# Batch 0's softmax ahead of the first weight conversions, and exponentials by head on ScalarE, in a fused attention and two-FFN kernel

## The chip, the cores and the metric

The program runs on one core of a Trainium2 chip. A core has TensorE (PE in the profile; its weight loads are PEld), VectorE (DVE), ScalarE (ACT), GpSimd (POOL) and SyncE (SP), which here issues the DMAs. Each engine works through its own instructions in a fixed order. The metric is the device time of one execution in microseconds (us), the median of several runs.

## The reference

Three stages, one behind the other, in float32. An attention over 8 batches, 8 heads, 576 positions and 64 values per head, in which the keys and values are first averaged over groups of eight positions; then a feed-forward layer with a leaky ReLU; then a gated feed-forward layer behind an RMS norm.

```python
k_p = k.reshape(B, H, Sp, pool, D).mean(axis=3)          # Sp = 72
v_p = v.reshape(B, H, Sp, pool, D).mean(axis=3)
scores = scale * np.matmul(q, k_p.transpose(0, 1, 3, 2))
scores = scores - np.max(scores, axis=-1, keepdims=True)
attn = np.exp(scores)
attn = attn / (np.sum(attn, axis=-1, keepdims=True) + 1e-09)
return np.matmul(attn, v_p)
...
h = x @ w_in                      # 4608 tokens, 512 -> 2048
g = np.maximum(0.01 * h, h)
return g @ w_out                  # 2048 -> 512
...
xn = x / np.sqrt(np.mean(x * x, axis=-1, keepdims=True) + 1e-06) * rms_g
g = xn @ w_gate                   # 512 -> 1536
return (g / (1 + np.exp(-g)) * (xn @ w_val)) @ w_out2
```

The weights arrive as float64.

## The kernel before

**Products.** Every large product is made of three TensorE products: each operand is split into a high part, rounded to a shorter float format, and a low part, the rest. `split` (L89 to L95) makes the two: a copy on ScalarE (L92) and a subtraction on VectorE or GpSimd (L95).

**Attention.** A batch has five tiles of queries (`t` = 0 to 4). Of each tile, step `t` transposes the queries (`qt`, `qT`), step `s` makes the scores and the softmax, step `x` transposes the softmax to `at` and `atr`, and the steps `av0` and `av1` multiply by the pooled values and write the tokens `xhl`. The steps `kp` and `vp` pool keys and values (`vs`, masked to `vm`, split to `vb`).

In `step_s` (L313) the scores of four heads stand in one PSUM bank (`sc`, two buffers under the tag `att`), 288 columns. For each half VectorE takes the maximum of each head (L331) and subtracts it (L332). Then one ScalarE instruction makes the exponentials of all eight heads, 576 columns (L336), VectorE sums them (L337), adds the small constant (L338), takes the reciprocal (L339) and multiplies (L340).

**Weights of the first layer.** `Weights` loads each 512 KB piece as pairs of 32-bit words (`raw_i` of w_in, `raw_o` of w_out) and makes a float of them. `begin` does one pass on ScalarE (L139, by the helper at L98) and one on VectorE (L141); `end`, one step later, combines the two on VectorE (L149) and splits the result (L92, L95; the subtraction on GpSimd for one piece, on VectorE for the next). A call of `W1.step` ends one piece and begins the next. Pieces are loaded into slots that earlier data leave. The last eight pieces, half as large, go through three buffers (tag `raw`) that batch 1's keys and values pass through too.

**First layer.** The 4,608 tokens are 9 tiles of 512, of which tile `j` = 0 holds batch 0. For each of 16 blocks `f` of w_in, `h_unit` (L597) makes `h` with 12 matmuls per 512 columns, then ScalarE makes `ghl` and `g` and VectorE their difference (L605); `y_unit` (L611) multiplies by w_out. Tile 0 runs its first 256 columns for `f` = 0 to 7, then all 512 columns for `f` = 8 to 15, then the other 256 columns for `f` = 0 to 7. Attention of the next batches and conversions run beside it.

**What sets the order.** In the first layer a scheduler that goes by its own timeline orders each engine's queue; the order written in the source is only one of its inputs. `keep_in_program_order` ties an instruction behind the one that was written just before it on its engine. In the second layer the written order is kept.

Of the kernel before, what the change touches and what calls it, by code (L numbers as in the profile page):

```python
# [8 lines left out]
F32 = mybir.dt.float32  # L9
# [3 lines left out]
AF = mybir.ActivationFunctionType  # L13
ALU = mybir.AluOpType
AX = mybir.AxisListType
# [7 lines left out]
def pooled_attention_then_two_ffns(  # L23
# [13 lines left out]
    nc = tc.nc  # L37
    B, H, S, D = q.shape
    NT, DM = out.shape
    P = 128  # L40
# [22 lines left out]
    ESCALE = 1.0 / (POOL * float(D) ** 0.5)  # L63
# [33 lines left out]
    def prelu(out, in_, alpha, scale=1.0):  # L97
        return nc.scalar.activation(out=out, in_=in_, func=AF.Prelu, scale=scale, alpha=alpha)  # L98
# [8 lines left out]
    class Weights:  # L107
# [25 lines left out]
        def begin(self):  # L133
            x = self.loaded.pop(0)
            t = x[2]
            top, low = t[:, :, 1], t[:, :, 0]


            prelu(top.bitcast(F32), top.bitcast(F32), 2.0 ** 32, scale=2.0 ** -112)  # L139

            nc.vector.tensor_scalar(  # L141
                out=low, in0=low.bitcast(U32), scalar1=0.9374 * 2.0 ** -29, scalar2=None, op0=ALU.mult
            )
            self.begun.append(x)

        def end(self):
# [22 lines left out]
    ap = att.__enter__()  # L169
# [5 lines left out]
    for h, sign in ((0, -1), (1, 1)):  # L175
        nc.gpsimd.affine_select(
            out=mask_main[:, h:h + 1], in_=mask_main[:, h:h + 1], compare_op=ALU.is_ge, fill=0.0,
# [4 lines left out]
    for sign, base in ((1, 0), (-1, REST - 1)):  # L182
        nc.gpsimd.affine_select(
            out=group, in_=group, compare_op=ALU.is_ge, fill=0.0, base=base, channel_multiplier=sign,
# [4 lines left out]
        out=mask_rest[:, :, 1], in_=group.rearrange("p d q -> p q d"), axis=AX.X, op=ALU.add  # L189
# [58 lines left out]
    def v_prep(b, r):  # L248
        rest = r >= NP
        n = R3 if rest else P  # L250
        x = vraw.pop((b, r))[0:n]
        vs = ap.tile([P, D], F32, tag="vs", bufs=2, name=f"vs{b}_{r}")[0:n]
        if b == 0:
            nc.vector.tensor_reduce(
                out=vs, in_=x.rearrange("p (r d) -> p d r", r=POOL), axis=AX.X, op=ALU.add
            )
        else:
            pool_sum(x)
            nc.gpsimd.tensor_tensor(out=vs, in0=x[:, 0:D], in1=x[:, D:2 * D], op=ALU.add)
        m = mask_rest.rearrange("p q h -> p (q h)") if rest else mask_main  # L260
        c = m.shape[1]
        vm = ap.tile([P, 4, D], F32, tag="vm", bufs=1, name=f"vm{b}_{r}")[0:n, 0:c]
        nc.gpsimd.tensor_tensor(
            out=vm, in0=vs.unsqueeze(1).to_broadcast([n, c, D]),
            in1=m.unsqueeze(2).to_broadcast([n, c, D]), op=ALU.mult,
        )
        if rest:

            t = ap.tile([R3, 4, D], F32R, tag="vbr", bufs=2, name=f"vb{b}_{r}")
            nc.scalar.activation(out=t, in_=vm, func=AF.Copy)  # L270
            z = slice(2 * R1, 3 * R1)
            nc.vector.tensor_tensor(out=t[z], in0=vm[z], in1=t[z].bitcast(F32), op=ALU.subtract)
        else:
            t = ap.tile([P, 2, 2, D], F32R, tag="vb", bufs=4, name=f"vb{b}_{r}")
            split(nc.scalar, t[:, HI], nc.vector, t[:, LO], vm)
        vb[b, r] = t
# [36 lines left out]
    def step_s(b, t):  # L313
        y = qT.pop((b, t))
        if b == 0:
            e = per.tile([P, H, SP], F32, tag=f"w{20 + t % 4}", bufs=1, name=f"ex{b}_{t}")
        else:
            e = ap.tile([P, H, SP], F32, tag="ex", bufs=1, name=f"ex{b}_{t}")
        st = ap.tile([P, 3, H], F32, tag="st", bufs=2, name=f"st{b}_{t}")
        n = 2 * SP  # L320
        for half in range(2):
            pt = bank("att", 2, f"sc{b}_{t}_{half}")
            for i in range(2):
                p = 2 * half + i
                nc.tensor.matmul(  # L325
                    pt[:, i * n:(i + 1) * n], y[:, p, :], kblk[b % 2][:, p * n:(p + 1) * n],
                    start=True, stop=True,
                )
            s = pt[:, 0:2 * n].rearrange("p (h c) -> p h c", h=4)
            hs = slice(4 * half, 4 * half + 4)  # L330
            nc.vector.tensor_reduce(out=st[:, 0, hs], in_=s, axis=AX.X, op=ALU.max)  # L331
            nc.vector.tensor_tensor(  # L332
                out=e[:, hs, :], in0=s, in1=st[:, 0, hs].unsqueeze(2).to_broadcast([P, 4, SP]),
                op=ALU.subtract,
            )
        nc.scalar.activation(out=e, in_=e, func=AF.Exp, scale=ESCALE)  # L336
        nc.vector.tensor_reduce(out=st[:, 1, :], in_=e, axis=AX.X, op=ALU.add)  # L337
        nc.vector.tensor_scalar(out=st[:, 1, :], in0=st[:, 1, :], scalar1=1e-9, scalar2=None, op0=ALU.add)  # L338
        nc.vector.reciprocal(out=st[:, 2, :], in_=st[:, 1, :])  # L339
        nc.vector.tensor_tensor(  # L340
            out=e, in0=e, in1=st[:, 2, :].unsqueeze(2).to_broadcast([P, H, SP]), op=ALU.mult
        )
        ex[b, t] = e
# [236 lines left out]
        W1.load()  # L580
    for x in before:
        run_step(x)
        if x[0] in "sx" and x[2] > 0:
            W1.step()

    gp = {}
# [675 lines left out]
```

## Time and profile before

| | |
|---|---|
| median of 3 runs | 1808.96 us (1805.79 to 1812.09) |
| the profiled execution | 1812.26 us, of which the span from first to last instruction is 1810.5 us |
| PE busy | 1758.0 us, 97% of the span |
| DVE, ACT, POOL busy | 891.1, 670.4, 551.2 us |

The page divides the span into 40 slices of 45 us. PE is busy for three tenths of the first and eight tenths of the second, and nine or more in all others, while DVE is at seven and nine tenths in these two and near five later. What is not TensorE's work therefore lies mostly in the first 90 us, and that stretch has to be read for itself.

### The profile page before, as it was taken

The page shows a single profiled execution, that of the slowest core. Times are in us where ns is not written, and L with a number is a line of the kernel's source. Part 1 is how long each engine was busy: PE and PEld are TensorE (multiplying, and loading weights), DVE is VectorE, ACT ScalarE, POOL GpSimd, SP SyncE. Part 2 cuts the span into 40 slices and gives each one's busy share as a digit, 9 for nine tenths or more (in the row PEclk, how much of TensorE's full clock was granted, in tenths as well). Part 3 has the DMA queues.
Part 4 walks back from the last instruction along what each step waited for, and adds up shares of the span by engine and source line. Part 5 has one row for each costly group of instructions (what it writes and reads, how often), then busy time and mean ns, then how long its engine had stood idle before and what let it go on. Part 6 is the DMA issues. An engine that isn't in the chain of part 4 may idle for free.

```text
span 1810.5 us, 23634 instructions
## 1 busy us (share of the span) xinstructions
PE 1758.0 (97%) x8596; PEld 1498.0 (83%) x8596; DVE 891.1 (49%) x1603; ACT 670.4 (37%) x1424; POOL 551.2 (30%) x681
## 2 busy tenths in 40 slices
PE   3899999999999999999999999999999999999999
PEld 2889887878888888888888888899788889978887
DVE  7974435454356555455344345345534444553331
ACT  5754333443344444344343332243232323322220
POOL 2653303334125142211110442154144204413320
PEclk6999999999999999999999999999999999999999
DMA  8833204447365555435451766687775668776562
GB/s 253 307 109 89 55 21 143 157 140 230 101 189 157 163 157 162 145 125 180 157 172 45 234 195 211 228 300 245 255 245 196 193 226 314 245 250 224 186 209 93
DMA packets 175555, 330.81 MB, mean 183 GB/s; under 512 B 54352, under 2 KB 90192, under 8 KB 174928
## 3 DMA queue, kind: packets, MB, share of 16 engines
q1 hardware_dynamic: 175440, 329.31, 56.1%
q8 instruction: 68, 1.11, 0.3%
q14 instruction: 47, 0.39, 0.1%
HBM read 277.87 MB, written 51.38 MB: 182 GB/s over the span
## 4 chain that ended last, share of the span: by engine, by line
PE 89%; DVE 5%; DMA 3%; issue 1%; ACT 1%; SPq 1%; POOL 1%; ACTq 0%; DVEq 0%; POOLq 0%
PE y L628 20%; PE h L592 20%; PE o L1089 16%; PE yg L1014 6%; PE yv L1014 6%; PE xv L1014 4%; PE xg L1014 4%; PE wg L1014 4%; PE wv L1014 4%; PE sc L325 2%; PE av L395 1%; PE xt L369 1%; DMA wo<-wo 1%; PE qt L303 1%; DMA y<-ye 1%
## 5 line engine op out<-in xcount | busy, mean ns | idle before, releaser
L592 PE MATMUL h<-xhl,w_i 128*128 128x512 f32 (+1 forms) x1824 | 438.2, 385 | 3.1 <-ACT xhl L92 1.3
L592 PEld LDWEIGHTS h<-xhl,w_i 128*128 128x128 f32 x1824 | 329.5, 191 | 68.3 <-DVE xhl L95 4.1
L1089 PE MATMUL o<-wo,u 128*128 128x512 f32 x1296 | 315.1, 390 | 3.5 <-DMA wo<-wo 3.4
L628 PE MATMUL y<-ghl,w_o 128*128 128x512 f32 (+1 forms) x1296 | 285.1, 365 | 1.4 <-DVE ghl L605 1.4
L1089 PEld LDWEIGHTS o<-wo,u 128*128 128x128 f32 x1296 | 242.0, 188 | 53.0 <-DMA wo<-wo 4.9
L628 PEld LDWEIGHTS y<-ghl,w_o 128*128 128x128 f32 x1296 | 218.9, 191 | 35.1 <-DVE ghl L605 1.8
L605 DVE TENSOR_TENSOR ghl<-g,ghl 128x512 fp32r<-128x512 f32 (+1 forms) x152 | 114.6, 754 | 241.5 <-ACT g L98 238.3
L98 ACT ACTIVATE ghl<-h 128x512 fp32r<-128x512 f32 (+1 forms) x152 | 87.0, 572 | 233.4 <-PE h L592 232.9
L628 PE MATMUL y<-ghl,wr 128*128 128x512 f32 x624 | 158.9, 395 | 0.0
L628 PEld LDWEIGHTS y<-ghl,wr 128*128 128x128 f32 x624 | 115.1, 188 | 22.4
L95 POOL TENSOR_TENSOR u<-e2g,u 128x512 fp32r<-128x512 f32 (+1 forms) x25 | 29.7, 1190 | 308.3 <-ACT u L92 308.3
L229 POOL TENSOR_TENSOR v<-v 128x256 f32<-128x256 f32 (+2 forms) x84 | 59.7, 713 | 107.6 <-DMA v<-in_v_dram 105.0
L98 ACT ACTIVATE g<-h 128x512 f32<-128x512 f32 (+1 forms) x152 | 86.8, 571 | 1.0 <-DVE ghl L605 1.0
L1014 PE MATMUL yg<-T,ag 128*128 128x512 f32 (+1 forms) x360 | 84.0, 368 | 0.0
L1014 PE MATMUL yv<-T,av 128*128 128x512 f32 (+1 forms) x360 | 83.8, 368 | 0.0
L1014 PE MATMUL xg<-xa,ag 128*128 128x512 f32 (+1 forms) x360 | 83.8, 367 | 0.0
L1014 PE MATMUL xv<-xa,av 128*128 128x512 f32 (+1 forms) x360 | 83.7, 367 | 0.0
L1014 PEld LDWEIGHTS yg<-T,ag 128*128 128x128 f32 x360 | 66.0, 188 | 10.0 <-DVE e1v L991 0.6
L1014 PEld LDWEIGHTS yv<-T,av 128*128 128x128 f32 x360 | 66.2, 188 | 9.5
L1014 PEld LDWEIGHTS xv<-xa,av 128*128 128x128 f32 x360 | 66.0, 188 | 9.6
L1014 PEld LDWEIGHTS xg<-xa,ag 128*128 128x128 f32 x360 | 66.1, 188 | 9.4
L735 POOL TENSOR_TENSOR parts_g<-raw_g,parts_g 128x256 fp32r<-128x256 f32 (+1 forms) x48 | 33.7, 727 | 102.7 <-ACT parts_g L731 102.7
(166 smaller groups left out, 2596.2 us busy)
## 6 DMA issues: line engine op xcount, KB each, us to landing
wo<-wo SPq DMA_DIRECT2D x120, 512.0 KB
av<-op_v SPq DMA_DIRECT2D x90, 512.0 KB
ag<-op_g SPq DMA_DIRECT2D x90, 512.0 KB
wr<-wo SPq DMA_DIRECT2D x52, 512.0 KB
y<-ye SPq DMA_DIRECT2D x36, 256.0 KB
op_g<-parts_g SPq DMA_DIRECT2D x36, 256.0 KB
op_v<-parts_v SPq DMA_DIRECT2D x36, 256.0 KB
out_dram<-oe SPq DMA_DIRECT2D x36, 256.0 KB
```

What stands on the lines that cost most here:

```text
L95: lo_eng.tensor_tensor(out=lo, in0=src, in1=hi.bitcast(F32), op=ALU.subtract)
L98: return nc.scalar.activation(out=out, in_=in_, func=AF.Prelu, scale=scale, alpha=alpha)
L229: nc.gpsimd.tensor_tensor(out=x[:, :n], in0=x[:, :n], in1=x[:, n:2 * n], op=ALU.add)
L303: nc.tensor.transpose(pt[:, c * P:(c + 1) * P], x[:, c * P:(c + 1) * P], ident)
L325: nc.tensor.matmul(pt[:, i * n:(i + 1) * n], y[:, p, :], kblk[b % 2][:, p * n:(p + 1) * n], start=True, stop=True,)
L369: nc.tensor.transpose(pt[:, c * P:(c + 1) * P], e[:, c, 0:P], ident)
L592: nc.tensor.matmul(pt, w[:, sp, c * P:(c + 1) * P], x[:, mp, c, :], start=c == 0 and i == 0, stop=c == n_k - 1 and i == 2,)
L605: nc.vector.tensor_tensor(out=t[:, LO, :], in0=g, in1=t[:, HI, :].bitcast(F32), op=ALU.subtract)
L628: nc.tensor.matmul(pt, w[:, sp, m * P:(m + 1) * P], g[:, mp, a - c0:a - c0 + n], start=ydone[j, a] == 1 and i == 0 and m % per_bank == 0, ...
L735: own(nc.gpsimd.tensor_tensor(out=d[:, :, LO, :], in0=x, in1=d[:, :, HI, :].bitcast(F32), op=ALU.subtract))
L1014: nc.tensor.matmul(pt, wt[:, a, c, sp, :], xt[:, mp, :], start=start and c == 0 and i == 0, stop=c == 1 and i == 2, skip_group_check=not s ...
L1089: nc.tensor.matmul(pt, u[:, sp, m * P:(m + 1) * P], w[:, mp, :], start=f == 0 and i == 0, stop=f == F2 - 1 and i == 2,)
```

## The change

There are three edits.

1. The two instructions of `begin` are tied behind what is written just before them on ScalarE and on VectorE. And `W1.step` is called behind other steps of batch 0: before, behind `s` of tile 1 and `x` of tile 1; now, behind `s` of tile 1, `x` of tiles 0 and 1 and each of the four `av0`, seven calls in all where there were two.
2. For batches 0 and 1 the subtraction, the single exponential and the sum are replaced. The maximum is scaled by -ESCALE (in two small VectorE instructions per tile), and ScalarE makes one exponential per head, 72 columns, straight from the scores, with that number as bias, and gives the head's sum as well.
3. `vs` has four buffers instead of two, `vm` two instead of one.

```diff
-            prelu(top.bitcast(F32), top.bitcast(F32), 2.0 ** 32, scale=2.0 ** -112)
+            x1 = prelu(top.bitcast(F32), top.bitcast(F32), 2.0 ** 32, scale=2.0 ** -112)
-            nc.vector.tensor_scalar(
+            x2 = nc.vector.tensor_scalar(
                 out=low, in0=low.bitcast(U32), scalar1=0.9374 * 2.0 ** -29, scalar2=None, op0=ALU.mult
             )
+            tc.keep_in_program_order(x1)
+            tc.keep_in_program_order(x2)
...
-        vs = ap.tile([P, D], F32, tag="vs", bufs=2, name=f"vs{b}_{r}")[0:n]
+        vs = ap.tile([P, D], F32, tag="vs", bufs=4, name=f"vs{b}_{r}")[0:n]
...
-        vm = ap.tile([P, 4, D], F32, tag="vm", bufs=1, name=f"vm{b}_{r}")[0:n, 0:c]
+        vm = ap.tile([P, 4, D], F32, tag="vm", bufs=2, name=f"vm{b}_{r}")[0:n, 0:c]
...
             nc.vector.tensor_reduce(out=st[:, 0, hs], in_=s, axis=AX.X, op=ALU.max)
+            if b < 2:
+                nc.vector.tensor_scalar(
+                    out=st[:, 0, hs], in0=st[:, 0, hs], scalar1=-ESCALE, scalar2=None, op0=ALU.mult
+                )
+                for i in range(4):
+                    h = 4 * half + i
+                    nc.scalar.activation(
+                        out=e[:, h, :], in_=s[:, i, :], func=AF.Exp, scale=ESCALE,
+                        bias=st[:, 0, h:h + 1], accum_out=st[:, 1, h:h + 1],
+                    )
+                continue
             nc.vector.tensor_tensor(
...
-        nc.scalar.activation(out=e, in_=e, func=AF.Exp, scale=ESCALE)
-        nc.vector.tensor_reduce(out=st[:, 1, :], in_=e, axis=AX.X, op=ALU.add)
+        if b >= 2:
+            nc.scalar.activation(out=e, in_=e, func=AF.Exp, scale=ESCALE)
+            nc.vector.tensor_reduce(out=st[:, 1, :], in_=e, axis=AX.X, op=ALU.add)
...
-        if x[0] in "sx" and x[2] > 0:
+        if x[0] in ("x", "av0") or x[0] == "s" and x[2] > 0:
             W1.step()
```

In the order of the instructions, three places. The first is VectorE at batch 0's first two tiles; `st_0` and `ex_0` belong to tile 0, `st_1` and `ex_1` to tile 1. Before:

```order
L141 TENSOR_SCALAR raw_i_0_119<-raw_i_0_119 128x512
L331 TENSOR_REDUCE st_1_213<-sc_1_0_214 128x4
L149 SCALAR_TENSOR_TENSOR raw_i_0_119<-raw_i_0_119 128x512
L254 TENSOR_REDUCE vs_4_259<-first_114 96x64
L331 TENSOR_REDUCE st_1_213<-sc_1_1_219 128x4
L332 TENSOR_TENSOR ex_1_212<-sc_1_0_214,st_1_213 128x288
L337 TENSOR_REDUCE st_0_196<-ex_0_195 128x8
L141 TENSOR_SCALAR raw_o_0_121<-raw_o_0_121 128x512
```

Now:

```order
L257 TENSOR_REDUCE vs_5_278<-first_123 96x64
L354 TENSOR_SCALAR st_0_196<-st_0_196 128x8
L334 TENSOR_REDUCE st_1_219<-sc_1_0_220 128x4
L355 RECIPROCAL st_0_196<-st_0_196 128x8
L275 TENSOR_TENSOR vb_4_275<-vm_4_273,vb_4_275 32x256
L337 TENSOR_SCALAR st_1_219<-st_1_219 128x4
L356 TENSOR_TENSOR ex_0_195<-ex_0_195,st_0_196 128x576
L275 TENSOR_TENSOR vb_5_282<-vm_5_280,vb_5_282 32x256
L334 TENSOR_REDUCE st_1_219<-sc_1_1_229 128x4
L337 TENSOR_SCALAR st_1_219<-st_1_219 128x4
L354 TENSOR_SCALAR st_1_219<-st_1_219 128x8
L355 RECIPROCAL st_1_219<-st_1_219 128x8
```

The first conversions (L141 of `raw_i_0`) stood among the two softmaxes, and now stand behind both; the sixth pooled value, `vs_5`, stands in front of tile 0's last softmax steps.

The second is ScalarE at tile 2 of batch 0, beside the first blocks of the first layer. Before:

```order
L92 ACTIVATE w_i_742<-raw_i_0_613 128x512
L98 ACTIVATE raw_o_0_403<-raw_o_0_403 128x512
L336 ACTIVATE ex_2_415<-ex_2_415 128x576
L98 ACTIVATE ghl_2_0_502<-h_2_0_488 128x256
L98 ACTIVATE g_2_0_501<-h_2_0_488 128x256
L92 ACTIVATE w_o_663<-raw_o_0_403 128x512
```

Now:

```order
L98 ACTIVATE raw_i_0_143<-raw_i_0_143 128x512
L311 COPY qT_4_569<-qt_4_564 128x512
L342 ACTIVATE ex_2_459,st_2_460<-sc_2_0_461,st_2_460 128x72 x4
L98 ACTIVATE ghl_2_0_560<-h_2_0_546 128x256
L342 ACTIVATE ex_2_459,st_2_460<-sc_2_1_470,st_2_460 128x72 x4
L98 ACTIVATE g_2_0_559<-h_2_0_546 128x256
L92 ACTIVATE w_i_448<-raw_i_0_143 128x512
```

One instruction became eight, and `ghl_2` and `g_2` of the first layer stand among them.

The third is VectorE at batch 1's second tile, whose transposed softmax (`at_0` from `xt_1`) TensorE needs for the product with the values; `raw_o_256` is one of the eight small last pieces. Before:

```order
L605 TENSOR_TENSOR ghl_12_0_1265<-g_12_0_1264,ghl_12_0_1265 128x512
L141 TENSOR_SCALAR raw_o_256_1423<-raw_o_256_1423 128x256
L149 SCALAR_TENSOR_TENSOR raw_o_256_1423<-raw_o_256_1423 128x256
L95 TENSOR_TENSOR at_0_1166<-xt_1_1359,at_0_1166 128x4x128
L378 TENSOR_TENSOR atr_0_1167<-xr_1_1366,atr_0_1167 32x2x128
```

Now:

```order
L621 TENSOR_TENSOR ghl_9_0_1049<-g_9_0_1048,ghl_9_0_1049 128x512
L152 SCALAR_TENSOR_TENSOR raw_o_0_815<-raw_o_0_815 128x512
L95 TENSOR_TENSOR at_0_1238<-xt_1_1438,at_0_1238 128x4x128
L95 TENSOR_TENSOR w_o_931<-raw_o_0_815,w_o_931 128x512
L141 TENSOR_SCALAR raw_i_0_871<-raw_i_0_871 128x512
```

The split of that tile stood behind a small last piece and behind block 12 of the first layer; now it stands behind block 9, ahead of all small pieces.

## Rows read from the trace of the kernel before

**Rows 1.** Windows: us, then PE, PEld, DVE, ACT, POOL busy (instructions), PEclk, DMA share, GB/s.

```profile
20.00:50.00 30.00, 12.76 (x64) 11.41 (x65) 29.15 (x56) 20.40 (x42) 10.42 (x9) 0.55 0.90 274
...
51.00:81.00 30.00, 25.52 (x203) 24.14 (x202) 29.62 (x57) 21.47 (x57) 19.76 (x27) 1.00 0.88 318
...
119.00:129.00 10.00, 7.29 (x34) 6.70 (x33) 6.99 (x15) 5.89 (x15) 4.76 (x10) 0.66 0.34 109
...
140.00:1800.00 1660.00, 1649.40 (x7952) 1402.05 (x7951) 771.50 (x1380) 584.87 (x1217) 484.00 (x580) 1.00 0.56 180
```

**Rows 2.** Timeline of DVE: start, us, instruction, [idle before <- releaser]; the first 100 us.

```profile
19.41 0.43 DVE L141 TENSOR_SCALAR raw_i<-raw_i 128x512 int32<-128x512 uint32 x1 [2.48 <-DMA raw_i<-in_moe_w_in_dram]
...
25.51 1.01 DVE L254 TENSOR_REDUCE vs<-first 96x64 f32<-96x512 f32 x1 [0.18 <-POOL vm L263]
...
34.16 0.76 DVE L340 TENSOR_TENSOR ex<-ex,st 128x576 f32<-128x576 f32 x1
...
48.13 0.42 DVE L95 TENSOR_TENSOR xhl<-av,xhl 128x256 fp32r<-128x256 f32 x1
...
51.30 1.31 DVE L605 TENSOR_TENSOR ghl<-g,ghl 128x256 fp32r<-128x256 f32 x1 [0.15 <-ACT g L98]
...
80.61 0.62 DVE L605 TENSOR_TENSOR ghl<-g,ghl 128x256 fp32r<-128x256 f32 x1
```

**Rows 3.** Timeline of DVE: softmax steps back to back, in the first two tiles.

```profile
21.69 0.45 DVE L331 TENSOR_REDUCE st<-sc 128x4 f32<-128x288 f32 x1
22.05 0.45 DVE L332 TENSOR_TENSOR ex<-sc,st 128x288 f32<-128x288 f32 x1
22.41 0.74 DVE L337 TENSOR_REDUCE st<-ex 128x8 f32<-128x576 f32 x1
23.07 0.90 DVE L141 TENSOR_SCALAR raw_o<-raw_o 128x512 int32<-128x512 uint32 x1
```

**Rows 4.** Timeline of DVE: a conversion's steps back to back.

```profile
39.51 0.43 DVE L141 TENSOR_SCALAR raw_o<-raw_o 128x512 int32<-128x512 uint32 x1
39.87 0.68 DVE L149 SCALAR_TENSOR_TENSOR raw_i<-raw_i 128x512 int32<-128x512 int32 x1
40.47 0.68 DVE L95 TENSOR_TENSOR w_o<-raw_o,w_o 128x512 fp32r<-128x512 f32 x1
```

**Rows 5.** L338 to 120 us (ns min/median/max), and one of it beside POOL.

```profile
L338 DVE TENSOR_SCALAR st<-st x7: 151/286/1282, 24.5 to 106.1; 128x8 f32<-128x8 f32 x7
...
90.41 0.95 DVE L338 TENSOR_SCALAR st<-st 128x8 f32<-128x8 f32 x1
...
90.02 1.32 POOL L95 TENSOR_TENSOR w_i<-raw_i,w_i 128x512 fp32r<-128x512 f32 x1 [0.47 <-ACT w_i L92]
```

**Rows 6.** ACT by form: count, busy us, mean ns; first 20 to 100 us, then whole.

```profile
L336 ACT ACTIVATE ex<-ex 128x576 f32<-128x576 f32 x6 | 4.1, 682 | 4.2 <-DVE ex L332 4.2
...
L98 ACT ACTIVATE g<-h 128x512 f32<-128x512 f32 x136 | 80.7, 593 | 1.0 <-DVE ghl L605 1.0
...
L860 ACT ACTIVATE rms<-ms,eps 128x512 f32<-128x512 f32 x6 | 4.1, 689 | 2.2 <-PE ms L857 2.1
```

**Rows 7.** Timeline of ACT: two weight passes, and eight copies of 72 columns or fewer.

```profile
38.65 0.65 ACT L98 ACTIVATE raw_o<-raw_o 128x512 f32<-128x512 f32 x1
39.21 0.69 ACT L98 ACTIVATE raw_i<-raw_i 128x512 f32<-128x512 f32 x1
...
72.21 1.40 ACT L295 COPY kblk<-kt 64x72 f32<-64x72 f32 x8
```

**Rows 8.** Timeline of PE: first y of block 8, an h, and the stop after 119 us.

```profile
97.61 0.74 PE L628 MATMUL y<-ghl,w_o 128*128 128x256 f32 x4
98.18 2.91 PE L592 MATMUL h<-xhl,w_i 128*128 128x512 f32 x12
...
122.85 1.01 PE L395 MATMUL av<-at,vb 128*128 128x256 f32 x3 [2.71 <-DVE at L95]
```

**Rows 9.** Timeline of DVE just before that stop's end.

```profile
120.47 0.85 DVE L141 TENSOR_SCALAR raw_o<-raw_o 128x256 int32<-128x256 uint32 x1 [5.11 <-POOL v L229]
```

## The prediction

> **What bounds the kernel now.** I read the page's slices first (PE is short of work in the first two only), then windows over the start, then the timelines of DVE, ACT and PE in them. From 140 to 1800 us PE is busy for 1649.4 of 1660 us: the change can win at most 10.6 us there, and its instructions are not there, except as the scheduler's order shifts. The start is another matter. From 20 to 50 us DVE is busy for 29.15 of 30 us and PE for 12.76, at a granted clock of 0.55; from 51 to 81 us DVE is busy for 29.62 of 30 and PE for 25.52 [rows 1]. So until about 81 us the end is set by DVE, and a microsecond taken from DVE's queue there is worth about one microsecond, until another engine is as full. ACT, at 21.47 of 30 us, is the next.
>
> **Part 1: the conversions behind the softmax.** DVE first stands for 2.48 us for a weight's load at 19.41 us, with batch 0's softmax queued behind it; tile 1's last softmax step ends at 34.9 us and the last piece of the tokens (`xhl`) starts at 48.13 us [rows 2]. In the new order no conversion stands ahead of that last softmax step. What then holds DVE is `vs_5`, whose load is queued behind the first two weights'. That load's end is not shown. It lies behind the first weight's, 19.4 us, and ahead of 25.3 us, when `vs_5` waited for GpSimd alone (25.51 less 0.18) [rows 2]; I take the middle, 22.4 us, and keep 3 us either way. From there: `vs_5` 1.0 [rows 2]; add, reciprocal and two scalings at 0.15 each, 0.6 [rows 5]; two maxima 0.7 [rows 3]; a multiply 0.7 [rows 2] and two small splits of about 0.4 (0.42 for `xhl` [rows 2]); then four exponentials, 1.4 (priced below), two copies 0.4, add and reciprocal 0.3 and the second multiply 0.7. That is 6.6 us, and the step ends at 29.0 instead of 34.9: 5.9 us gained. From there to the last `xhl`, DVE has 9 first steps (L141), 8 combines (L149) and 3 splits of weights before, and 6, 5 and 2 now. Starts lie 0.36, 0.60 and about 0.60 apart [rows 4], so 3.5 us go; tile 0's two splits come in at 1.0, one small split of 0.4 goes: 2.9 us. **8.8 us** earlier, with 5.8 and 11.8 as ends.
>
> The seven conversions less are work deferred, not saved: they come back in the next stretch.
>
> **Part 2: exponentials by head.** Per tile DVE loses two subtractions at 0.36 and one sum at 0.66 [rows 3] and gains two scalings. The nearest row, L338, takes 0.15 at least, 0.29 in the middle and 1.28 at most; at 90.41 us it took 0.95 and ended with the GpSimd instruction that had begun at 90.02 [rows 5]. So DVE gains 1.1 us per tile with free scalings, and loses 0.5 with two that are held as that one was.
>
> (The Trainium skill, "SBUF — State Buffer", section "Who interferes with whom", says that tensor_scalar can take the port pair that DVE shares with GpSimd and then waits for a whole GpSimd instruction, while tensor_reduce never contends. That speaks against this trade, and 90.41 us agrees with it; with all eight scalings of the next stretch held for that long, DVE would need 6.4 us more there, 41.3, and the sum would be 3.4 us less: 1803.0.)
>
> ACT takes eight exponentials of 72 columns in place of one of 576, which took 0.68 [rows 6]. No row shows a small one with bias and sum. Eight copies of 72 columns took 1.40 us, 0.175 each [rows 7]; a bias operand added 0.10 (689 against 593 ns) [rows 6]; reading out the sum costs something from nothing to another such instruction, 0.175. So p lies between 0.27 and 0.45; I take the middle, **0.36**, since neither end has a nearer row. A tile costs ACT 2.2 us more.
>
> (The Trainium skill, "ScalarE: Activation LUTs", section "What ACT_TABLE_LOAD costs", gives 280 ns and 0.833 ns per column with a bias operand, of which 93 ns overlap: an estimate of 0.25 us for 72 columns. The trace agrees on the bias. By 0.25 ACT would need 34.4 us in the stretch below and not be the bound; the page does not price the sum.)
>
> **The next stretch,** from block 0's `ghl` (51.30 us) to block 7's (80.61), took 29.3 us [rows 2]. Counted between the same two instructions in the new order, DVE has 4 more first steps (1.4), 4 more combines (2.4), 1 more split (0.6), 2 more maxima (0.7), 8 scalings (1.2), an add and a reciprocal (0.3) and twelve small splits of batch 0's last token steps (2.9, from 0.42 for the largest), and 6 subtractions (2.2) and 3 sums (2.0) less: 29.6 + 5.3 = 34.9 us. ACT has 7 more weight passes at 0.56 [rows 7] (3.9), seventeen more small pieces at about 0.175 (3.0), three large exponentials less (2.0) and 32 small ones: 21.5 + 4.9 + 32p = 26.4 + 32p, which is 37.9 us, between 35.0 and 40.8. So **ACT takes DVE's place**, and the stretch lasts 37.9 instead of 29.3: 8.6 us given back. Two engines this full also wait for each other, since each exponential waits for DVE's maximum and each multiply for ACT's sum, and `ghl_2` stands among exponentials. I take 2 us for that; zero to 4 is open.
>
> What is done by then is more. Before, 17.0 us passed from there to the first y of block 8 at 97.61 [rows 2, 8]. Now batch 0's second half is already through, and PE needs ten matmuls of y (256 columns, half of an h matmul's 0.24, 1.2 us), block 8's h (2.9) [rows 8], two matmuls of block 9 (0.5) and ten small ones for batch 1 at about 0.18 (1.8): 6.4 us. Ten matmuls of block 9 are still to come, which were done before: 2.4. So 17.0 - 8.8 = 8.2 us come back.
>
> **Part 3: more buffers.** `vs` and `vm` let GpSimd pool ahead. DVE waited 0.18 us for it [rows 2], and PE's wait at that place was for tokens. I cost it at nothing: DVE's and ACT's work covers it; without that cover it is worth the 0.18.
>
> **The stop at 120 us.** DVE stood 5.11 us at the conversion of a small last piece, behind a load that waited for one of the three shared buffers [rows 9]; queued behind it was batch 1's `at` split, for which PE stood 2.71 us [rows 8]. The clock followed: 0.66 over 119 to 129 us, while it is 1.00 from 51 to 81 [rows 1]. A mean of 0.66 over 10 us is 6.8 us at half speed, 3.4 lost. The stop costs 6.1 us. In the new order that split stands four blocks earlier, ahead of all small pieces, so this stop cannot come in this form. But batch 1's `vb_4` now stands among the last pieces, and PE's product with it stands ahead of block 15's y. I take half, **3.0 us**, with 0 and 6.1 as ends.
>
> **The sum.** 8.8 - 8.6 - 2.0 + 8.2 + 3.0 = 9.4 us. Against the profiled execution, 1812.3, that is 1802.9; that execution lay 3.3 us above the median of the runs, which is what is compared, so 1808.96 - 9.4 = **1799.6 us**. What the scheduler's new order does behind 140 us cannot be costed; with 10.6 us of PE idle there, I allow 3 us either way.
>
> **The rivals.** (a) *DVE stays the bound.* If p is 0.27, both engines need 35 us; without mutual waiting, and with the 120 us stop gone whole: 8.8 - 5.7 + 8.2 + 6.1 = 17.4, 1791.6 us. For it: a copy of the same size takes 0.175, and DVE's 34.9 is what is left as the bound. Against: no row has the sum.
>
> (b) *ScalarE takes back what VectorE gave.* p 0.45 and 2 us of mutual waiting make the stretch 42.8 us; with the stop replaced by its like at `vb_4`, 8.8 - 13.5 + 8.2 + 0 = 3.5 us, 1805.5: nothing that can be measured. The like comes from DVE if all eight scalings are held as at 90.41 us: 41.3 us instead of 34.9. For it: 32 new instructions on an engine that was already at 72%.
>
> (c) *PE's clock falls in that stretch, slower.* PE's work there grows from 25.5 us by sixteen matmuls of 320 columns (under 0.24 each [rows 8]) and some transposes, to about 31 us in 40: 78% busy against 85% at full clock before. If its stops for ACT keep the clock at half, as from 20 to 50 us [rows 1], PE itself becomes the bound. With a share s of the stretch at half clock it lasts 31/(1 - s/2): up to s = 0.45 nothing is lost; at s = 0.74 it lasts 49.2 and the gain is gone; at s = 0.85 it is 53.9, 14 us more than forecast, 1813.6, and beyond that measurably slower, 1815 at s = 0.88. Against it: PE stayed at 1.00 from 51 to 81 us although it stood for 4.5 us of them [rows 1].
>
> (d) *The tie does not order.* The order shows it does; what stays is that the deferred conversions could come too late for blocks 8 to 15. PE needs 5.8 us per block there and DVE about 3 (two first steps, two combines, one split and a `ghl`), so I give it no chance of its own.
>
> **How the numbers follow.** About 0.3% (5.4 us) is what a measurement of this kernel can tell from no change: faster is below 1803.5, slower above 1814.4. Forecast 0.42 (its own range 1796 to 1803.4), (a) 0.22, (b) 0.25, (c) 0.11. So faster 0.64, same 0.25, slower 0.11. The range leaves out (c) and the outer half of (a)'s order noise: 1790 to 1808.
>
> **What would show it.** Block 0's `ghl` on DVE at about 42.5 us instead of 51.3, block 7's near 82; ACT busy above 90% between them where it was 72%; exponentials of 72 columns 0.36 us apart; scalings of 0.15 us with a few held by GpSimd; the first y of block 8 near 89 us; no DVE wait of 5 us behind a small piece with PE idle. Wrong would be a `vs_5` that starts behind 25 us, exponentials above 0.45 us apart, DVE still full while ACT has room, or a PE stop with half clock behind 100 us.

## The result, and the profile after

The changed kernel takes **1835.24 us** (median of 4 runs, 1833.8 to 1837.42) where the kernel before took 1810.46 in the runs beside it: a ratio of 1.0141, with a 95% interval of 1.0124 to 1.0159. It is 25 us slower. The prediction was 1799.6 us, with a range of 1790 to 1808.

The page of the changed kernel, which is read first:

```profile
span 1833.6 us, 23800 instructions
...
PE 1766.3 (96%) x8596; PEld 1501.7 (82%) x8596; DVE 863.4 (47%) x1593; ACT 688.3 (38%) x1574; POOL 543.3 (30%) x681
...
PE   4797899999999999999999999999999999999999
...
PEclk7999899999999999999999999999999999999999
```

Before, only the first two slices of 45 us were short of TensorE work. Now the first shows 4 tenths instead of 3, the second 7 instead of 8, and the fourth and fifth (some 137 to 229 us) show 7 and 8 where there was a 9, with a lower clock in the fifth. The loss lies behind the stretch that the change was about. Windows of the changed kernel, the first four as in [rows 1] (us, then PE, PEld, DVE, ACT, POOL busy, PEclk, DMA share, GB/s), then three more:

```profile
20.00:50.00 30.00, 18.68 (x106) 16.91 (x105) 22.39 (x44) 19.31 (x62) 9.39 (x11) 0.60 0.97 301
51.00:81.00 30.00, 23.33 (x174) 21.19 (x174) 25.67 (x58) 25.66 (x95) 16.42 (x23) 1.00 0.75 254
119.00:129.00 10.00, 10.00 (x60) 8.83 (x59) 6.91 (x15) 6.39 (x14) 2.58 (x3) 1.00 0.14 43
140.00:1800.00 1660.00, 1632.08 (x7828) 1385.94 (x7828) 759.38 (x1390) 595.10 (x1272) 490.27 (x602) 0.99 0.56 181
...
140.00:160.00 20.00, 15.99 (x117) 15.50 (x117) 7.52 (x18) 6.97 (x23) 12.12 (x25) 0.91 0.31 95
160.00:180.00 20.00, 16.93 (x143) 16.69 (x142) 8.78 (x18) 10.33 (x51) 8.85 (x18) 1.00 0.35 89
180.00:200.00 20.00, 10.67 (x37) 8.47 (x38) 6.82 (x17) 8.85 (x37) 11.45 (x24) 0.51 0.49 144
```

From 140 us on PE stands for 27.9 us where it stood for 10.6, and 16.4 of these lie between 140 and 200 us, with about half the clock in the last 20. Nothing of the kind was there before: the three windows from 140 to 200 us showed PE busy for 59.89 of 60 us. The stop at 120 us is gone (10.00 of 10 us busy).

VectorE's timeline of the changed kernel, answering [rows 2]:

```profile
22.83 1.01 DVE L257 TENSOR_REDUCE vs<-first 96x64 f32<-96x512 f32 x1 [4.89 <-DMA first<-in_v_dram]
...
28.81 0.76 DVE L356 TENSOR_TENSOR ex<-ex,st 128x576 f32<-128x576 f32 x1
29.48 0.42 DVE L141 TENSOR_SCALAR raw_i<-raw_i 128x512 int32<-128x512 uint32 x1
...
45.60 0.95 DVE L621 TENSOR_TENSOR ghl<-g,ghl 128x256 fp32r<-128x256 f32 x1
...
86.45 0.43 DVE L621 TENSOR_TENSOR ghl<-g,ghl 128x256 fp32r<-128x256 f32 x1
...
119.11 0.42 DVE L141 TENSOR_SCALAR raw_o<-raw_o 128x512 int32<-128x512 uint32 x1
...
123.19 0.29 DVE L141 TENSOR_SCALAR raw_i<-raw_i 128x256 int32<-128x256 uint32 x1
```

The first conversion stands behind the softmax (29.48 us instead of 19.41), and block 0's `ghl` comes 5.7 us earlier. Block 7's comes 5.8 us later. The first small last piece is converted at 123.19 us; in the kernel before:

```profile
107.90 0.28 DVE L141 TENSOR_SCALAR raw_i<-raw_i 128x256 int32<-128x256 uint32 x1
```

Why that matters is read from SyncE's queue, of which no row stood in the prediction (`v` x3 at L217 are the loads of a batch's last two pooled values, `v_4` and `v_5`):

```profile
72.40 2.00 SPq L130 DMA_DIRECT2D raw_i<-in_moe_w_in_dram  x2
...
75.01 0.55 SPq L213 DMA_DIRECT2D v<-in_v_dram  x1
...
91.84 0.33 SPq L213 DMA_DIRECT2D v<-in_v_dram  x1
...
129.27 2.00 SPq L217 DMA_DIRECT2D v<-in_v_dram  x3
...
139.21 1.99 SPq L217 DMA_DIRECT2D v<-in_v_dram  x3
```

In the kernel before, the first small pieces (`raw_i` x2) are loaded at 96.21 us, `v_4` at 91.83, ahead of them, and `v_5` at 111.86:

```profile
91.83 2.00 SPq L214 DMA_DIRECT2D v<-in_v_dram  x3
95.61 0.35 SPq L130 DMA_DIRECT2D raw_o<-in_moe_w_out_dram  x1
96.21 0.88 SPq L130 DMA_DIRECT2D raw_i<-in_moe_w_in_dram  x2
...
111.86 1.98 SPq L214 DMA_DIRECT2D v<-in_v_dram  x3
```

Now the small pieces are loaded at 72.40 us, ahead of `v_1` to `v_5`, and hold two of the three shared buffers for 50 us. `v_4` and `v_5` come 37 and 27 us later. TensorE's stops that follow, in the changed kernel:

```profile
151.75 0.50 PE L416 MATMUL av<-atr,vb 96*128 96x256 f32 x2 [2.64 <-DVE vb L275]
...
171.59 0.37 PE L608 MATMUL h<-xhl,w_i 128*128 128x256 f32 x1
183.35 1.11 PE L385 MATMUL xt<-ident,ex 128*128 128x128 f32 x4 [6.42 <-ACT qT L311]
...
198.23 2.33 PE L608 MATMUL h<-xhl,w_i 128*128 128x512 f32 x5
```

The product with the values waits for the split of `v_5` (`vb`) at 151.75. The last `h` matmul of tile 0 runs at 171.59, and tile 1 can't start before batch 1's tokens: its first `h` is at 198.23. In the kernel before it is at 176.88:

```profile
176.88 2.92 PE L592 MATMUL h<-xhl,w_i 128*128 128x512 f32 x12
```

In between, once tile 0's last `y` matmuls are done, TensorE has only batch 1's late attention, step by step, and nothing to fill the steps with. That is 21 of the 23 us by which the two profiled executions differ (1833.6 less 1810.5), and it is never made up.

### The profile page after: what moved, and what is told of

It is laid out like the page before. It is cut to its first block, busy times and chain, and to the rows that moved or that the text cites. A ratio compares the mean times of both kernels' runs of the same rounds, so it can differ in the third digit from the quotient of the medians.

```text
span 1833.6 us, 23800 instructions
## 1 busy us (share of the span) xinstructions
PE 1766.3 (96%) x8596; PEld 1501.7 (82%) x8596; DVE 863.4 (47%) x1593; ACT 688.3 (38%) x1574; POOL 543.3 (30%) x681
## 4 chain that ended last, share of the span: by engine, by line
PE 82%; DMA 6%; POOL 4%; DVE 2%; issue 2%; ACT 2%; SPq 1%; POOLq 0%; ACTq 0%; DVEq 0%
PE h L608 17%; PE y L644 17%; PE o L1105 15%; PE yg L1030 6%; PE yv L1030 6%; PE xg L1030 4%; PE xv L1030 4%; PE wg L1030 4%; PE wv L1030 4%; DMA v<-in_v_dram 2%; PE sc L328 2%; DMA y<-ye 1%; POOL v L232 1%; PE av L411 1%; DMA wo<-wo 1%
## 5 line engine op out<-in xcount | busy, mean ns | idle before, releaser
L608 PE MATMUL h<-xhl,w_i 128*128 128x512 f32 (+1 forms) x1824 | 442.8, 387 | 5.7 <-ACT xhl L92 2.2
L621 DVE TENSOR_TENSOR ghl<-g,ghl 128x512 fp32r<-128x512 f32 (+1 forms) x152 | 108.1, 711 | 230.6 <-ACT g L98 230.1
L95 POOL TENSOR_TENSOR u<-e2g,u 128x512 fp32r<-128x512 f32 (+1 forms) x25 | 29.6, 1183 | 307.5 <-ACT u L92 307.5
L232 POOL TENSOR_TENSOR v<-v 128x256 f32<-128x256 f32 (+1 forms) x84 | 56.3, 670 | 128.5 <-DMA v<-in_v_dram 118.9
```

The costliest lines, as they stand in the source:

```text
L95: lo_eng.tensor_tensor(out=lo, in0=src, in1=hi.bitcast(F32), op=ALU.subtract)
L232: nc.gpsimd.tensor_tensor(out=x[:, :n], in0=x[:, :n], in1=x[:, n:2 * n], op=ALU.add)
L608: nc.tensor.matmul(pt, w[:, sp, c * P:(c + 1) * P], x[:, mp, c, :], start=c == 0 and i == 0, stop=c == n_k - 1 and i == 2,)
L621: nc.vector.tensor_tensor(out=t[:, LO, :], in0=g, in1=t[:, HI, :].bitcast(F32), op=ALU.subtract)
```

## Experiments

After the trace three theories stood. **M**: the small pieces, loaded early and converted late, delay batch 1's values. **A**: the exponentials by head load ScalarE and make the two engines wait for each other. **T**: the tie itself, which makes conversions wait in written order. All ratios are to the kernel before, with a 95% interval; 0.001 is 1.8 us.

### The order of the loads

**e_gate**: the changed kernel with the small pieces held back.

```diff
-    W1 = Weights(todo1, lambda x: (8 if x[0][1] < 6 else 4) if x[1].stop - x[1].start == 512 else 2)
+    W1 = Weights(todo1, lambda x: (8 if x[0][1] < 6 else 4) if x[1].stop - x[1].start == 512 else 2 if (1, 4) in vb else 0)
```

> The changed kernel, with one difference: the eight small last weight pieces are not loaded before the fifth pooled value of batch 1 (v_4) has been taken, as it was in the kernel before; the tie, the seven calls, the exponentials by head and the buffers stay. Theory M (buffers): in the changed kernel the first two small pieces are loaded ahead of v_1 at 72 us, are converted only at 123 us, and hold two of the three shared buffers for that time, so that v_1 to v_5 pass through one; batch 1's attention comes 20 us late and runs into the border of tiles 0 and 1. By M this kernel has vb_4 and vb_5 of batch 1 ready before 125 us, no PE stop of several us near 150 and 183 us, full clock from 180 to 200 us, tile 1's first h near 176 instead of 198 us, and takes 1800 to 1812 us. Theory A (ScalarE): the eight exponentials per tile of batch 1 and the two engines' mutual waits make the loss; then it stays at 1828 to 1840. Theory T (tie): conversions held in written order make it; then also 1828 to 1840.

Measured: 1816.08 us, 1.0043 (1.0027 to 1.0060). Some 18 of the 25 us are back. Its windows:

```profile
140.00:160.00 20.00, 20.00 (x160) 19.64 (x159) 8.84 (x21) 10.55 (x46) 13.95 (x28) 0.97 0.43 119
160.00:180.00 20.00, 20.00 (x170) 19.88 (x168) 9.66 (x20) 11.96 (x53) 13.90 (x28) 1.00 0.51 146
180.00:200.00 20.00, 19.49 (x97) 16.18 (x97) 11.26 (x29) 9.88 (x27) 9.15 (x16) 1.00 0.24 70
```

Its loads of `v_4` and `v_5`, and tile 1's first `h`:

```profile
80.15 2.00 SPq L217 DMA_DIRECT2D v<-in_v_dram  x3
...
124.25 1.99 SPq L217 DMA_DIRECT2D v<-in_v_dram  x3
...
181.48 3.04 PE L608 MATMUL h<-xhl,w_i 128*128 128x512 f32 x12
```

The hole is closed, with the tie, the exponentials and the buffers still there, and tile 1 starts 17 us earlier than in the changed kernel. M holds for the greater part, though not for all of its forecast (1800 to 1812): `v_4` comes early here, but `v_5` still behind four small pieces.

**e_order**: edit 1 alone (the tie and the seven calls).

> The kernel before with edit 1 alone (the tie and the seven calls; no exponentials by head, old buffers). M: most of the loss is here, since the seven calls move the small pieces' loads ahead of v_1: 1822 to 1840 us, with v_4 of batch 1 loaded behind 120 us. A: no loss, 1800 to 1812. T: as M, 1822 to 1840, so this run tells M and T from A only.

1820.29 us, 1.0066 (1.0049 to 1.0082). About half of the loss is here without any exponential by head, with `v_4` loaded at 125.64 us: A falls as the only cause. The run came out just below M's band (1822).

**e_exp**: edit 2 alone.

> The kernel before with edit 2 alone (exponentials by head in batches 0 and 1). M and T: within 8 us of before, 1802 to 1817 us, batch 1's loads at before's times. A: most of the loss is here, 1825 to 1840, with ScalarE above 90% busy from 51 to 81 us and batch 1's at late.

1809.98 us, 1.0006 (0.9995 to 1.0018): nothing that can be measured. ScalarE is busy for 27.59 of the 30 us from 51 to 81, over 90% as A had it, and yet there is no loss. The exponentials by head cost nothing and win nothing by themselves.

**e_notie**: the changed kernel without the two `keep_in_program_order` lines.

> The changed kernel without the tie (the seven calls, exponentials and buffers stay). The small pieces are still loaded ahead of v_1. M: they still hold the buffers, but may be converted as soon as they are there; if they are converted by 100 us the loss is gone (1800 to 1815), if they wait until 120 us it stays (1825 to 1840); what decides is the time between a small piece's load and its conversion, and v_4's load follows it. T: without the tie 1800 to 1812 even where the small pieces hold their buffers as long. A: 1828 to 1840.

1820.80 us, 1.0067 (1.0049 to 1.0084), between the two cases written down. The first small pieces are converted at 87 and 91 us, but `v_4` stands in SyncE's queue behind others, and `v_5` is loaded at 123.84:

```profile
113.68 2.00 SPq L215 DMA_DIRECT2D v<-in_v_dram  x3
```

TensorE stands for 7.0 of the 60 us from 140 to 200 here, and for 0.1 at most with edit 2 alone (e_exp) or edit 3 alone (e_buf, below). So the calls seem to delay batch 1's values without the tie as well. That is argued, since no run has the calls alone, nor edits 2 and 3 together without them. The tie made the other 13 us of the changed kernel.

**e_tie_exp**: tie and exponentials, but the two old calls and the old buffers.

```diff
-        if x[0] in ("x", "av0") or x[0] == "s" and x[2] > 0:
+        if x[0] in "sx" and x[2] > 0:
```

> The kernel before with the tie and the exponentials by head, but with the two old calls of the conversion step and the old buffers. The small pieces are then written and loaded behind v_4, as before. If it is the seven calls that put the small pieces ahead of v_4 and so make the loss, there is no stop near 150 and 180 us here and the time is 1800 to 1810. If the tie makes the loss by itself, since conversions wait in written order: 1818 to 1830.

1812.05 us, 1.0020 (1.0007 to 1.0034), 2 us above the band for "the calls make it" and 6 below the other. Against the same kernel with the seven calls (e_oldbuf, next, 1.0092) this is the calls' price beside the tie: 1.0092 less 1.0020, some **13 us**. They put five more calls of `W1.step` into batch 0, and the small pieces' loads with them, ahead of `v_1`. Here the first small piece is converted as late as 119.77 us, and that costs little, since `v_4`'s load stands ahead of it (80.64 us). So late conversions alone do not make the loss; small pieces that are queued ahead of batch 1's values do, and the tie makes it larger (e_notie). Together the calls and the tie make 12 to 13 us (e_order, and this difference).

One number goes with the stop in all twenty kernels of this document, the kernel before and the changed kernel among them. In the seven that load `v_4` behind 110 us (at 113.68 to 129.27), TensorE stands for 7.0 to 16.4 of the 60 us from 140 to 200. In the other thirteen (`v_4` at 78.18 to 100.45) it stands for 3.5 at most.

### The buffers

**e_oldbuf**: the changed kernel without edit 3.

> The changed kernel without edit 3 (vs two buffers, vm one). Edits 1 and 2 alone made +11.7 and +1.4 us, the whole +26. If edit 3 is worth nothing in it, 1830 to 1840. If it is edit 3 that adds the missing 13 us, since v loads run ahead of what needs the shared buffers, 1818 to 1825.

1825.89 us, 1.0092 (1.0070 to 1.0115), just above the lower of the two bands. Edit 3, which the prediction put at zero, costs 1.0141 less 1.0092, **9 us**. Part of it is seen before 40 us. VectorE's timeline of e_oldbuf:

```profile
18.50 0.75 DVE L356 TENSOR_TENSOR ex<-ex,st 128x576 f32<-128x576 f32 x1
23.20 1.01 DVE L257 TENSOR_REDUCE vs<-first 96x64 f32<-96x512 f32 x1 [3.95 <-DMA first<-in_v_dram]
...
26.68 0.76 DVE L356 TENSOR_TENSOR ex<-ex,st 128x576 f32<-128x576 f32 x1
...
39.64 0.43 DVE L621 TENSOR_TENSOR ghl<-g,ghl 128x256 fp32r<-128x256 f32 x1
```

The wait for the sixth pooled value's load is nearly the same; its place is not. With two `vs` buffers tile 0's softmax is through (18.50) before VectorE stands. With four, that value is put ahead of it, and tile 0's last softmax step comes at 24.98. Block 0's `ghl` is at 39.64 instead of 45.60, and tile 1's first `h` at 190.27 instead of 198.23, so the lead is kept that far.

**e_buf, e_vs4, e_vm2**: the kernel before with edit 3, with `vs` in four buffers only, and with `vm` in two only.

> The kernel before with edit 3 alone (vs four buffers, vm two). In the changed kernel edit 3 costs 9 us, since with four vs buffers the sixth pooled value, whose load ends near 22.8 us, is put ahead of tile 0's last softmax steps and VectorE stands 4.9 us with them behind it. In the kernel before conversions fill VectorE until then, so no such loss should be seen: within 4 us of before. If more buffers cost by themselves (GpSimd pooling ahead and holding VectorE's steps): 1814 to 1820.

> The kernel before with vs in four buffers, vm in one. Edit 3 as a whole made +8.5 us on the kernel before. If vs alone makes it (the sixth pooled value is put earlier in VectorE's order, and later pooled values run ahead): 1815 to 1821, with vm2 within 4 us of before.

> The kernel before with vm in two buffers, vs in two. If vm makes edit 3's +8.5 us (GpSimd masks ahead, so that VectorE's and ScalarE's splits of v come in another place): 1815 to 1821; otherwise within 4 us of before.

1818.41 us (1.0047, 1.0030 to 1.0064), 1836.88 (1.0155, 1.0140 to 1.0170) and 1819.39 (1.0059, 1.0044 to 1.0074). So edit 3 costs 8.5 us on the kernel before as well, against my expectation of within 4, and its halves do not add: `vs` alone costs 28 us, `vm` alone 10.7. Its 8.5 us here are not those of the changed kernel: in e_buf block 0's `ghl` is only 1.4 us later than before (52.68), TensorE works through all of 140 to 200 us, and no wait of it behind 100 us is longer than 3.0. For `vs` alone, two of TensorE's waits in e_vs4:

```profile
193.31 1.19 PE L628 MATMUL y<-ghl,w_o 128*128 128x512 f32 x4 [2.96 <-ACT ghl L98]
...
716.00 4.21 PE L592 MATMUL h<-xhl,w_i 128*128 128x512 f32 x9 [10.48 <-ACT xhl L92]
```

At 716 us a tile's first `h` waits 10.48 us for its tokens, a border where the kernel before had no such wait (its longest `h` wait there was 1.32 us at 694). The number of buffers changes the scheduler's plan, and not in batch 0 alone: this stop comes at 716 us. Why its plan meets the border badly with one number and less so with another stays open.

**e_raw4**: e_oldbuf with four shared buffers for keys, values and small pieces (`bufs=3` to `bufs=4` in three places).

> The same with a fourth shared buffer for keys, values and small pieces (it fits only without edit 3, so it is compared with the kernel without edit 3). Theory M, that the number of buffers that the small pieces hold is what delays v_4 and v_5: 1810 to 1825, v_4 and v_5 loaded before 110 us. If it is the loads' place in SyncE's queue, behind weights' loads that wait for conversions, and not the number of buffers: within 4 us of that kernel.

1826.92 us, 1.0103 (1.0087 to 1.0119), no different from e_oldbuf. Its loads of `v_4` and `v_5`:

```profile
124.82 2.00 SPq L217 DMA_DIRECT2D v<-in_v_dram  x3
...
134.47 1.98 SPq L217 DMA_DIRECT2D v<-in_v_dram  x3
```

So theory M was wrong in one half: one buffer more does not help, since the small pieces ahead of `v_4` in SyncE's queue take it as well; their *place* there delays `v_4`. Three more of them stand between `v_3` and `v_4`, and wait for buffers that come free by conversions at 121 us and later. A number of buffers that holds all the small pieces was not run.

### Two other suspects

**e_b0**: exponentials by head in batch 0 alone (`b < 1`).

> The changed kernel with exponentials by head in batch 0 only; batch 1 has subtraction, one exponential and sum as before. If batch 1's exponentials add the 13 us that edits 1 and 2 alone don't explain (eight instructions in ScalarE's queue behind each late tile, and tile 0's y copies between them): 1817 to 1826, and no half clock over the whole of 180 to 200 us. If not: 1830 to 1840.

1833.24 us, 1.0136 (1.0120 to 1.0152): as the changed kernel. Batch 1's exponentials are not it.

**e_ystore**: tile 0's y stores issued from ScalarE's queue.

```diff
-                nc.sync.dma_start(
+                (nc.scalar if j == 0 else nc.sync).dma_start(
                     out=y_dram[j][:, m * per_bank:(m + 1) * per_bank, a:a + n],
```

> The changed kernel with tile 0's four y stores issued from ScalarE's queue instead of SyncE's. In the changed kernel the first of them stands in SyncE's queue behind a key load that waits for a buffer (4.8 us), ScalarE's next y copy waits 6.7 us for it, and TensorE stands 6.4 us at 183 us behind ScalarE's qT, with half clock to 200 us. If that queue makes the stop: 1822 to 1830, no stop above 3 us near 183. If batch 1's late attention makes it anyway, through its own waits: 1831 to 1839, with a stop of another name.

1834.81 us, 1.0139 (1.0123 to 1.0156): no change. The stop has another time and the same name,

```profile
180.41 1.11 PE L385 MATMUL xt<-ident,ex 128*128 128x128 f32 x4 [5.15 <-ACT qT L311]
```

so SyncE's queue ahead of the y stores was not what set the end, although the y store is what the trace names behind ScalarE's wait. That batch 1's attention is late, with nothing beside it, is left; e_gate shows it from the other side.

### Without the two causes

**e_gate_notie** (held-back pieces, no tie), **e_gate_oldbuf** (held-back pieces, no edit 3), **e_gate_tie4** (the same with the tie for blocks 0 to 3 alone).

> The changed kernel with the small pieces held back until v_4 of batch 1 is taken, and without the tie. The held-back loads alone gave 1816.1 us, 7.5 above before. Theory T2 (the tie makes the rest: with it block 0's to block 7's ghl takes 41 us and no engine is full in it, since three engines wait for each other in a fixed order): 1804 to 1812, that stretch 30 to 36 us. Theory A2 (the exponentials, or the other buffers, make the rest): 1813 to 1819, whatever the stretch.

> The changed kernel without edit 3 and with the small pieces held back until v_4 of batch 1 is taken. Holding back gave 19 us in the changed kernel, leaving out edit 3 gave 9 us; the first acts between 140 and 200 us, the second before 40 us (block 0's ghl at 39.6 instead of 45.6). Theory I (two independent causes): they add, 1804 to 1810 us, block 0's ghl at 39 to 40 us and tile 1's first ghl at 181 to 186. Theory J (a gain of the first 40 us is given back later in any case, as the stretch from block 0 to block 7 did): 1813 to 1818.

> As e_gate_oldbuf, with the tie on the pieces of blocks 0 to 3 only. With the tie on all pieces blocks 8 to 15 of tile 0 took 44 to 48 us, without it 39 to 42 us. If that is the tie's doing, this kernel keeps block 0's ghl near 40 us and gains 3 to 6 us between blocks 8 and 15: 1799 to 1806. If the untied pieces are put ahead of the softmax or the tokens again, block 0's ghl is at 45 or later and the time 1806 to 1816.

1815.14 us (1.0031, 1.0020 to 1.0043), 1811.15 (1.0013, 1.0001 to 1.0025) and 1813.63 (1.0016, 1.0002 to 1.0030). The first is no different from e_gate (1.0043), though its stretch from block 0 to block 7 takes 35.2 us: with the small pieces held back the tie costs nothing that can be measured, and T2 falls. The second lies between the bands of I and J, nearer to I: holding back won 17.7 us and leaving out edit 3 8.9, and both together 23.1. The two causes nearly add, and with both out 2 us are left. It is also no gain, though block 0's `ghl` comes at 40.94 us instead of 51.30. The third has it at 43.16, and its blocks 8 to 15 take 41.3 us instead of 49.9, so that part is the tie's doing, and yet it is no better.

Why is a lead of 10 us not kept? In four kernels that were compared the 28 full pieces are converted at nearly one pace: from 19.41 to 104.75 us before, 3.16 us per piece; 3.32 in the changed kernel (29.48 to 119.11); 3.29 in e_exp and 3.18 in e_notie. What begins 10 us later ends 14 us later. Blocks 8 to 15, which need the last of them, take longer from block 8's `ghl` to block 15's: 41.9 us before, 47.0 in the changed kernel, 49.9 in e_gate_oldbuf. Tied pieces may be a chain through ScalarE and VectorE, which one step more between their halves would loosen:

**d_gate_oldbuf**:

```diff
-            if self.begun:
+            small = bool(self.loaded) and self.loaded[0][1].stop - self.loaded[0][1].start < 512
+            while self.begun and (len(self.begun) >= 2 or small or not self.loaded):
                 self.end()
```

> As e_gate_oldbuf (tie, seven calls, exponentials by head, old buffers, small pieces held back), with one step more between the two halves of a conversion: a step ends the piece begun two steps earlier, where it ended the piece begun last. In every kernel with the tie on all pieces the pairs of conversions start 5 to 6.5 us apart, from 27 us to the last, with exponentials by head or without, while VectorE has room behind 90 us. Theory K (the tied conversion is a chain: ScalarE's pass, VectorE's combine, ScalarE's copy, each waited for in written order): with the extra step pairs are closer, the first small piece is converted before 103 us, and the time is 1800 to 1808. Theory L (the pairs' pace is the sum of the work on VectorE and ScalarE): the pace stays and the time too, 1808 to 1815.

1816.57 us, 1.0040 (1.0028 to 1.0052). The pace went from 3.30 to 3.06 us per piece, the first small piece came at 114 us (103 in e_gate_oldbuf), and the kernel was slower. K falls as a way to gain. L, that the pace is the sum of VectorE's and ScalarE's work, forecast an unchanged pace and 1808 to 1815 us, and neither came. What sets the pace stays open.

**e_raw4b, e_exp_raw4**: four shared buffers on the kernel before, alone and with exponentials by head.

> The kernel before with a fourth shared buffer for keys, values and small pieces, and nothing else. It measures the stop at 120 us by itself: there VectorE stood 5.1 us at a small piece whose load waited for one of the three buffers, and TensorE 2.7 us with half clock behind it; the prediction priced the stop at 6.1 us. If that price holds: 1801 to 1805 us and no stop of TensorE between 118 and 130 us. If the next thing in the order makes a stop of its own, as in the kernels with held-back pieces (2.8 to 4.4 us at 126 to 131 us): 1806 to 1812.

> Exponentials by head (edit 2) and the fourth shared buffer, with neither the tie nor the seven calls nor edit 3. The best that the experiments point to: edit 2 alone was +1.4 us by its median and left VectorE room; by the stop's price 1800 to 1806. If the orders' later collisions eat it, as in all others: 1807 to 1815.

1812.61 us (1.0021, 1.0010 to 1.0032) and 1808.94 (0.9992, 0.9982 to 1.0001). In e_raw4b the stop at 120 us shrank, with full clock beside it,

```profile
122.61 0.62 PE L395 MATMUL av<-at,vb 128*128 128x256 f32 x3 [1.89 <-DVE at L95]
```

and nothing was won. Twelve executions of this one kernel took 1807.1 to 1817.4 us, and the profiled one was the fastest of them: one trace can't decide about 4 us here, and the medians do. No version beat the kernel before measurably.

## The prediction, step by step

**Part 1 held in its steps, not in its sum.** `vs_5` started at 22.83 us (22.4 forecast), and tile 1's softmax ended at 29.6 (29.0). Block 0's `ghl` came at 45.60, 5.7 us earlier, where 8.8 was forecast with 5.8 as the low end. The 3 us lie behind 29.5 us, where VectorE stood for 2.7 us in four waits for ScalarE, such as this one:

```profile
32.97 1.34 DVE L152 SCALAR_TENSOR_TENSOR raw_o<-raw_o 128x512 int32<-128x512 int32 x1 [0.96 <-ACT raw_o L98]
```

I counted VectorE's work there and took it for full; with fewer conversions in it, it waits between them.

**Part 2's prices were good, its conclusion was not.** Exponentials stood 0.295 us apart, within the bounds of 0.27 and 0.45 (0.36 taken). The stretch took 40.85 us (39.9 forecast), but not because ScalarE had become the bound. In it VectorE was busy for 35.23 us (34.9 forecast) and ScalarE for 35.36 (35.8 by the forecast's count at 0.295), so the counts were good and neither engine was full: 5.5 us are waits, where I took 2 and allowed 4. And e_order, without any small exponential, has the same stretch (44.15 to 85.07, 40.9 us):

```profile
51.00:81.00 30.00, 22.42 (x151) 19.86 (x152) 27.29 (x56) 20.96 (x58) 16.75 (x24) 0.94 0.75 266
```

There ScalarE is busy for 20.96 us, as before the change, and VectorE is the fuller engine. So ScalarE's load does not set the length of this stretch, and the number came out right by luck: a price of the exponentials that was too high stood in for waits that were too low. The scalings cost 0.17 us in the median and 0.78 at most.

**The credit of 8.2 us failed.** The first y of block 8 came at 95.84 us, not near 89, and TensorE waited for weights and for `ghl` on the way (0.84 us for a `w_i` at 94.39, 2.14 for `ghl` at 86.20). That is 1.8 us ahead of before, less the 2.4 us of block 9 still to come: nothing, where the terms up to here had promised 6.4.

**Part 3 was mis-sized.** Zero was forecast, with 0.18 us if its cover went; it cost 9 us. I looked for a wait that more buffers remove, and not for the order that they allow: the row of the wait (25.51) could not show that, but the new order of VectorE, which I quoted, did show `vs_5` ahead of tile 0's last steps.

**The stop at 120 us** went as forecast, and its like came back 30 us later as a larger one. I had named `vb_4` as the place of a like and let it cost no more than the old stop, so that the term's low end was 0. That cap had no row behind it. Nor was the old stop worth 6.1 us: with its cause alone lessened (e_raw4b) nothing was won.

**The rivals.** None was it. (c) had the right sign, but TensorE's clock stayed at 1.00 from 51 to 81 us and fell at 180. The step that failed most is in (d): "the deferred conversions could come too late" for blocks 8 to 15, given no chance since VectorE needs 3 us per block and TensorE 5.8. I counted engines and not what queues behind the pieces: the small ones hold buffers and stand in SyncE's queue ahead of batch 1's values. It is these that came too late (`v_4` at 129.27 us instead of 91.83), and holding the small pieces back gave 18 of the 25 us back. And behind 140 us I allowed 3 us either way because PE was idle for 10.6 us there. That bounds a gain. It bounds no loss, and it was there that the loss was.

In sum, from the ratios: tie and exponentials 3.6 us (e_tie_exp), the calls beside the tie 13, edit 3 9, which are the 25.5 measured, since each is a difference to the next. Each also holds whatever else the scheduler reordered between two kernels, which can be much: `vs` alone makes 28 us. The three edits each alone make 11.9, 1.1 and 8.5 us, 21.5 together; 4 us belong to none of them alone.

## What to carry to other kernels

Of a step that is moved earlier, follow every load that it issues to what is queued behind it, and every buffer that it takes to when it is given back; a load that comes earlier without its consumer coming earlier holds its buffer and delays the loads queued behind it for longer. Where a stretch is nearly full, its idle time caps what can be won there and says nothing about what can be lost. And where a scheduler makes the order, a number of buffers is a change of order: read the new order at each place where it differs, and price it as a reordering, not as room.

## What the runs showed of the hardware

An exponential with a sum is two instructions on ScalarE. The timeline of ScalarE in the changed kernel:

```profile
17.57 0.32 ACT L342 ACTIVATE ex<-sc,st 128x72 f32<-128x72 f32 x1 [2.49 <-DVE st L337]
17.79 0.19 ACT L342 ACTIVATION_READ_ACCUMULATOR ex<-sc,st 128x1 f32 x1
17.88 0.31 ACT L342 ACTIVATE ex<-sc,st 128x72 f32<-128x72 f32 x1
```

Pairs start 0.30 us apart, and the reading takes some 0.09 of it (17.79 to 17.88). The estimate of 0.25 us in the prediction, from the Trainium skill ("ScalarE: Activation LUTs", section "What ACT_TABLE_LOAD costs"), is without that reading; with 0.09 added it is above what was measured.

The granted clock of the first 50 us differed between kernels with the same early order: from 20 to 50 us it was 0.60 in the changed kernel and 1.00 in e_b0, with block 0's `ghl` at 45.60 and 45.70 us and TensorE busy for 18.68 and 18.16 us. The window of e_b0:

```profile
20.00:50.00 30.00, 18.16 (x107) 16.21 (x107) 22.30 (x44) 18.93 (x60) 9.29 (x11) 1.00 0.99 312
```

In this stretch TensorE was not the bound, and the lower clock cost nothing that the `ghl` shows.
